# Tile 0 of a fused attention and feed-forward kernel split into 6 and 10 slices instead of 8 and 8

## The chip, the cores and the metric

The kernel runs on one core of a Trainium2 chip. The metric is the device time of one execution in microseconds (us). A core has a matrix engine (TensorE, PE in the profile, with its weight loads as PEld), a vector engine (VectorE, DVE), an engine for activation functions and copies (ScalarE, ACT), a general engine (GpSimd, POOL) and a queue that issues all transfers here (SyncE, SP). Each works through its own instructions in order and waits on semaphores for the others. PE writes into eight PSUM banks.

## The reference, cut to what matters

```python
# attention: 8 batches, 8 heads, 576 positions, 64 wide, float32
scores = q @ k.transpose / sqrt(64)
scores = where(mask, scores, -1e9)     # heads 0-3: the last 32 keys; heads 4-7: every 4th of the last 128
attn = exp(scores - max); attn = attn / (sum + 1e-9)
x = (attn @ v)                          # laid out as (4608 tokens, 512)
# feed-forward, w_in (512, 2048) and w_out (2048, 512) in float64
h = x @ w_in
g = max(h, 0) + alpha * min(h, 0)
out = g @ w_out                         # float32
```

Products run at float32 accuracy on PE by splitting each operand into a high and a low part: three passes (high by high, high by low, low by high) in place of one. The float64 weights are turned into such pairs of float32 on the core.

## The kernel before, in words

**Tiles, slices, pairs, chunks.** The 4608 tokens are nine tiles of 512. The 2048 hidden features are 16 slices of 128. For tile t and slice f, `ffn_h` (12 matmuls, L340) makes h, an activation makes g, and `ffn_y` (12 matmuls, L387) adds g times a slice of w_out into four PSUM banks `y`, one for each block of 128 outputs. Attention goes by pairs of heads: four pairs a batch, `pairs[0]` to `pairs[31]`. A pair's steps are `scores` (72 small matmuls, L185), `maxima` (DVE, L193 and L196), `exponentials` (ACT, nine, L203), `divisions` and `turns` (DVE, L210 to L218), `values` (76 small matmuls, L231), then `highs` (ACT) and `lows` (DVE), which put x in its tile as high and low part. Batches are 576 tokens, so that tile 0 needs the four pairs of batch 0, and tile 1 those of batches 0 and 1. A chunk is one slice of w_in or w_out, 512 KB as float64: `load_weight` on SP's queue, `magnitude` on ACT (L307), four `words` on DVE (L313 to L319), `high` on ACT (L325) and `low` on DVE (L328). There are 32, in the order of the list `wq`; `load` and `conversion` take the next of it.

**Stages.** Each engine's order is that in which the code below emits. (1) L784 to L853: the first loads, the four pairs of batch 0 (loop over `s`), with one chunk converted a round, and the start of tile 0. (2) The loop over `n` up to `CUT`, 8: tile 0's slices 0 to 7, with the four pairs of batch 1 and pairs of chunks; a pair's scores and maxima stand in one slice and its division in the next, so that a pair takes two slices. Seventeen chunks are through when it ends. The half sums of tile 0 go to memory (`part`). (3) The loop from `CUT` to `NS` (48): tile 1's 16 slices, with one chunk each, then tile 0's slices 8 to 15, then tile 2 in two halves. Slice n emits h of the slice after it and y of the slice before it. From slice 20 on every second slice scores a pair of batch 2 and later; from slice 24 (`SECOND`) the weights are saved to memory (`save`), and POOL adds up parts of them (`combine`, L431 and L434) in the space of tile 1's x, at its first call from slice 25, once tile 1's last h has read that space. At slice 32 tile 0's second half ends: the four partial sums are loaded, added on DVE (L395) and written out. (4) `paired_stage`: tiles 3 to 8 by twos, from about 370 us on.

**Activation.** `ffn_relu` (ACT, two operations, L348 and L349) and `ffn_sum` (DVE, L354) up to tile 1's end; after that `ffn_parts` (two DVE operations, L361 and L362). `ffn_high` and `ffn_low` split g.

**Shared space.** Scores, values and h take the four PSUM banks `a0` to `a3` in turn, so that a bank is free again when what it held four banks ago has been read. `y` takes the other four. Staged chunks and g share five buffers by turns (`gbuf`); chunks 4 to 15 are staged where the weights of slices 8 and 9 will lie, and the pairs of batches 0 and 1 lie where those of slices 10 to 15 will. Activations, magnitudes and outputs share five buffers with the tag `m`.

Of the kernel before, what the change touches and what calls it, by code (L numbers as in the profile page):

```python
# [37 lines left out]
CUT = 8  # L38
# [12 lines left out]
def tile_window_attention_prelu_ffn(  # L51
# [49 lines left out]
    SPANS = ((0, CUT), (CUT, CUT + 2), (CUT + 2, NF))  # L101
# [177 lines left out]
    def load_weight(which, f):  # L279
        i = order[which, f]  # L280
        if NC <= i < 2 * CUT:
            st = spare_st[i % 4]
        else:
            st = gbuf([P, DM, 2], U32, f"ws{which}_{f}")
# [7 lines left out]
    class Conversion:  # L292
# [7 lines left out]
        def magnitude(self):  # L300
            i = self.index
            if NC <= i < 2 * CUT and i % 2 == 0:
                self.a = spare_a[i // 2 % 2]
            else:
                self.a = ffp.tile([P, DM], U32, tag="m", name=f"wa{self.id}", bufs=5)

            nc.scalar.activation(out=self.a.bitcast(F32), in_=self.st[:, :, 1].bitcast(F32), func=AF.Abs)  # L307
# [66 lines left out]
    def ffn_y(t, f):  # L374
        first = (t, f) in ((0, 0), (0, CUT), (1, 0), (2, CUT))
# [4 lines left out]
        last = cut or (t, f) in ((0, NF - 1), (1, NF - 1), (2, CUT - 1))  # L380
# [10 lines left out]
        if not last:  # L391
            return
        for c in range(NC):
            if rest:
                nc.vector.tensor_tensor(out=o[c], in0=ys[t][c], in1=o[c], op=ALU.add)  # L395
            elif c % 2:
                nc.vector.tensor_copy(out=o[c], in_=ys[t][c])
            else:
                nc.scalar.copy(out=o[c], in_=ys[t][c])  # L399
            nc.sync.dma_start(  # L400
                out=part[c] if cut else outT[c * P:(c + 1) * P, t * TT:(t + 1) * TT], in_=o[c])
# [393 lines left out]
    pairs[3].load_v()  # L795
    pairs[0].scores()
    pairs[1].scores()
    for s in range(NC):
# [3 lines left out]
        if s == 0:  # L802
# [6 lines left out]
            for op in w.words():  # L809
                op()  # L810
        else:
# [20 lines left out]
    v.maxima(w.words())  # L832
    now = [conversion(), conversion()]
    words = [op for ops in zip(*(w.words() for w in now)) for op in ops]
    for op in words[:4]:
        op()
# [5 lines left out]
    for op in words[4:]:  # L842
        op()
    w.high()
    w.low()
# [11 lines left out]
    score_at = {2 * i + 1: pairs[NC + 1 + i] for i in range(NC - 1)}  # L857
    turn_at = {2 * i: pairs[NC + i] for i in range(NC)}
    value_at = {2 * i + 1: pairs[NC + i] for i in range(NC)}
    for p in range(2 * NC, AHEAD):  # L860
        n = EARLY + 2 * (p - 2 * NC)
        score_at[n] = pairs[p]
        turn_at[n + 2] = pairs[p]
        value_at[n + 3 if p == 2 * NC else n + 2] = pairs[p]
    divide_at = {n + 1: u for n, u in score_at.items()}

    for n in range(CUT):


        scored, valued, turned = score_at.get(n), value_at.get(n), turn_at.get(n)  # L870
        words = [op for ops in zip(*(w.words() for w in now)) for op in ops]
# [4 lines left out]
        if n + 1 == CUT:  # L876
            ffn_y(*slices[n - 1])
        if n == 0:
            for f in range(2):
                ffn_sum(*slices[f])  # L880
        elif turned:
            ffn_sum(*slices[n])
        ffn_high(*slices[n])
        if turned:
            turned.divisions()
            turned.turns()
        for w in late:
            w.low()
        if scored:
            scored.maxima([lambda: ffn_low(*slices[n])] + words)  # L890
            ffn_h(*slices[n + 1])
            scored.exponentials(0, 4)
            valued.highs()
            scored.exponentials(4)
            valued.lows()
        else:
            if valued:
                valued.highs()
                valued.lows()
            if n:  # L900
                ffn_h(*slices[n + 1])
            ffn_low(*slices[n])
            for op in words[:4]:
                op()
        following = None
        if turned:
            following = [conversion() for _ in range((2, 2, 2, 1, 0, 0, 1, 1)[n])]
            if n:

                ffn_relu(*slices[n + 1])  # L910
                ffn_sum(*slices[n + 1])
            for op in words[4:]:
                op()
        elif not scored:
            for op in words[4:]:
                op()
        late = now
        for _ in range((2, 2, 1, 0, 0, 1, 1, 1)[n]):
# [154 lines left out]
```

## Time and profile before

| what | us |
|---|---|
| median of 3 runs (901.9 to 904.94) | 902.15 |
| the profiled execution, its own time | 903.91 |
| its span | 901.0 |
| busy in the span: PE / DVE / ACT / POOL | 855.4 / 561.2 / 395.6 / 48.1 |
| mean clock granted to PE | 0.981 |

In the lists of the profile a row of a timeline gives the start in us from the span's beginning, the length, the engine, the line in the kernel, the operation with what it writes and reads, and in brackets the idle time ahead of it with what ended it. Neighbouring instructions are merged (x12), and lengths of merged rows overlap the next by the pipeline's depth; differences of starts are the better prices. A row of busy times gives a stretch, then its length and the busy time of each engine, then the granted clock (1.00 is full speed), the share of transfers and GB/s.

### The profile page before, as it was taken

What the parts mean: (1) busy time and instruction counts of PE and PEld (TensorE: products, weight loads), DVE (VectorE), ACT (ScalarE), POOL (GpSimd) and SP (SyncE); (2) the same over time, 40 slices, a digit from 0 to 9 for tenths busy, and PEclk for the clock granted to TensorE, in tenths of its full rate; (3) what the DMA queues carried; (4) which work ended last, traced back from release to release, by engine and by line L of the source; (5) the groups of instructions that cost most, each with busy time, mean ns of one, the idle gap of its engine ahead of it and who ended that gap; (6) DMA issues with size and microseconds to landing.
All of it is one profiled execution on the core that took longest, in us unless ns stands there. A gap on an engine that the chain in (4) does not pass through costs nothing.

```text
span 901.0 us, 19714 instructions
## 1 busy us (share of the span) xinstructions
PE 855.4 (95%) x8048; PEld 706.7 (78%) x8048; DVE 561.2 (62%) x962; ACT 395.6 (44%) x1122; POOL 48.1 (5%) x52
## 2 busy tenths in 40 slices
PE   4659999989998999999999999999999999999998
PEld 4547788868887878888888888888788888888886
DVE  5999688786666767676436666664357527404731
ACT  4666555534434354464335642563356216303610
POOL 0000000030222432000000000000000000000000
PEclk9769999998999999999999999999999999999999
DMA  9632253214798976475557565665466467435641
GB/s 331 217 130 79 70 172 102 95 54 155 225 305 255 305 230 191 165 201 151 165 167 194 173 199 159 203 176 142 115 179 173 140 175 193 135 94 166 185 129 47
DMA packets 101305, 151.82 MB, mean 168 GB/s; under 512 B 8416, under 2 KB 47328, under 8 KB 101216
## 3 DMA queue, kind: packets, MB, share of 16 engines
q1 hardware_dynamic: 101216, 150.58, 55.5%
q8 instruction: 63, 1.03, 0.5%
q14 instruction: 26, 0.21, 0.1%
HBM read 116.99 MB, written 33.55 MB: 167 GB/s over the span
## 4 chain that ended last, share of the span: by engine, by line
PE 87%; DVE 7%; ACT 2%; issue 1%; DMA 1%; SPq 1%; DVEq 0%; ACTq 0%
PE y L670 29%; PE pA L532 15%; PE h L340 13%; PE y L387 12%; PE pC L532 7%; PE o L231 4%; PE pB L532 4%; PE s L185 3%; DVE w_dt.float32r L328 1%; ACT w_dt.float L203 1%; DMA mask_sb<-masks 1%; DVE pt L218 1%; DVE wa L317 1%; DVE g L372 1%; DMA ob<-part 1%
## 5 line engine op out<-in xcount | busy, mean ns | idle before, releaser
L340 PE MATMUL h<-x,w_dt.float32r 128*128 128x512 f32 x576 | 146.5, 405 | 10.4 <-DVE w_dt.float L193 6.2
L387 PE MATMUL y<-g,w_dt.float32r 128*128 128x512 f32 x576 | 140.7, 394 | 0.0
L340 PEld LDWEIGHTS h<-x,w_dt.float32r 128*128 128x128 f32 x576 | 110.9, 195 | 35.1 <-DVE w_dt.float L193 6.5
L387 PEld LDWEIGHTS y<-g,w_dt.float32r 128*128 128x128 f32 x576 | 109.2, 190 | 23.5 <-ACT ob L399 0.4
L670 PE MATMUL y<-gp,ring_w 128*128 128x512 f32 x480 | 112.3, 391 | 0.0
L670 PEld LDWEIGHTS y<-gp,ring_w 128*128 128x128 f32 x480 | 89.8, 188 | 18.8
L670 PE MATMUL y<-gp,ring_xA 128*128 128x512 f32 x444 | 103.8, 391 | 0.0
L670 PEld LDWEIGHTS y<-gp,ring_xA 128*128 128x128 f32 x444 | 83.1, 188 | 17.5
L203 ACT ACTIVATE pr<-pr,nm 128x64 f32<-128x64 f32 x216 | 72.2, 336 | 47.7 <-DVE nm L196 47.7
L574 ACT COPY stage<-pA 128x512 f32<-128x512 f32 x72 | 42.3, 588 | 105.2 <-PE pA L532 105.2
L600 DVE TENSOR_TENSOR gp<-n,gp 128x512 fp32r<-128x512 f32 x96 | 63.2, 684 | 0.0
L592 DVE SCALAR_TENSOR_TENSOR n<-n,bal,stage 128x512 f32<-128x512 f32 x72 | 54.0, 749 | 13.9 <-ACT n L588 13.1
L367 ACT CAST g<-m 128x512 fp32r<-128x512 f32 x48 | 29.8, 621 | 68.7 <-DVE m L362 61.0
L532 PE MATMUL pA<-parts_w,ring_w 128*128 128x512 f32 x234 | 57.7, 390 | 0.8 <-ACT raw_xA L267 0.8
L596 ACT CAST gp<-n 128x512 fp32r<-128x512 f32 x96 | 56.6, 615 | 1.9 <-DVE n L592 1.9
L532 PE MATMUL pA<-parts_w,ring_xA 128*128 128x512 f32 x228 | 56.2, 390 | 0.5 <-ACT raw_xB L267 0.5
L670 PE MATMUL y<-gp,ring_g 128*128 128x512 f32 x228 | 54.5, 392 | 0.0
L693 DVE TENSOR_TENSOR ob<-y,py 128x512 f32<-128x512 f32 x24 | 16.4, 691 | 57.8 <-PE y L670 57.8
L532 PEld LDWEIGHTS pA<-parts_w,ring_w 128*128 128x128 f32 x234 | 43.9, 188 | 9.9 <-ACT raw_xA L267 0.9
L588 ACT ACTIVATE n<-stage 128x512 f32<-128x512 f32 x72 | 45.6, 634 | 12.5 <-DVE stage L581 12.0
L532 PEld LDWEIGHTS pA<-parts_w,ring_xA 128*128 128x128 f32 x228 | 42.7, 188 | 9.4 <-ACT raw_xB L267 0.6
L670 PEld LDWEIGHTS y<-gp,ring_g 128*128 128x128 f32 x228 | 42.5, 188 | 9.1
(97 smaller groups left out, 1148.8 us busy)
## 6 DMA issues: line engine op xcount, KB each, us to landing
ring_w<-wS SPq DMA_DIRECT2D x68, 256.0 KB, 2.9
ring_xA<-wS SPq DMA_DIRECT2D x67, 256.0 KB, 2.9
ring_w<-wO SPq DMA_DIRECT2D x40, 256.0 KB, 2.8
ring_xA<-wO SPq DMA_DIRECT2D x37, 256.0 KB, 2.8
out<-ob SPq DMA_DIRECT2D x36, 256.0 KB, 3.0
ring_g<-wS SPq DMA_DIRECT2D x33, 256.0 KB, 2.9
wO<-w_dt.float32r SPq DMA_DIRECT2D x32, 256.0 KB, 4.7
wS<-wc SPq DMA_DIRECT2D x16, 512.0 KB, 3.4
```

The source lines that it names most:

```text
L203: nc.scalar.activation(out=self.pr[:, r, :], in_=self.pr[:, r, :], func=AF.Exp, bias=self.nm[:, r:r + 1], scale=1.0, accum_out=self.sm[:, ...
L231: nc.tensor.matmul(self.po[u][e * D:(e + 1) * D, a:z, :], lhsT=self.v[rows, i, :], rhs=self.pt[rows, a * BK + (BQ if i else 0):z * BK - (B ...
L340: nc.tensor.matmul(ms[t, f], lhsT=weight(0, a, f)[:, c * P:(c + 1) * P], rhs=half(t, c)[:, e, :], start=(c == 0 and n == 0), stop=(c == NC ...
L367: nc.scalar.copy(out=g[:, 0, :], in_=ms[t, f])
L387: nc.tensor.matmul(ys[t][c], lhsT=weight(1, a, f)[:, c * P:(c + 1) * P], rhs=g[:, e, :], start=(first and n == 0), stop=(last and n == 2),)
L532: nc.tensor.matmul(to, lhsT=w[:, (2 * a + c) * P:(2 * a + c + 1) * P], rhs=part_of(name, e)[:, c * TT:(c + 1) * TT], start=start and c == ...
L574: nc.scalar.copy(out=self.s(n), in_=self.A)
L588: nc.scalar.activation(out=self.m[n], in_=self.at(n), func=AF.Relu, scale=-1.0)
L592: nc.vector.scalar_tensor_tensor(out=self.m[n], in0=self.m[n], scalar=bal[:, f:f + 1], in1=self.at(n), op0=ALU.mult, op1=ALU.add)
L596: nc.scalar.copy(out=self.g(n)[:, 0], in_=self.m[n])
L600: nc.vector.tensor_tensor(out=g[:, 1], in0=self.m.pop(n), in1=g[:, 0].bitcast(F32), op=ALU.subtract)
L670: nc.tensor.matmul(ys2[tt], lhsT=w[:, k * P:(k + 1) * P], rhs=g[:, e], start=j == 0 and n == 0, stop=j == GF - 1 and n == 2)
```

## The change

`CUT` becomes 6, and `HALF` = 8 takes its place wherever 8 stood for the storage of the weights, for tile 2's halves, for the saves and POOL's sums (`SCRATCH`), and for the first load of batch 2. So slices 0 to 5 are tile 0's first part, 6 to 21 tile 1, 22 to 31 tile 0's other ten; from slice 24 the slice numbers of saves, sums and pairs are those of before.

- The first chunk is loaded right behind the first pair's q and k and converted ahead of the first maxima; the masks come in two transfers, the second ahead of pair 3.
- The loop over tile 0's first slices is written anew: slice n scores pair 5 + n, takes its maxima, exponentials, division and turn, and slice n + 1 has its values. Chunks are taken by the list `taken`, one or two a slice; `ahead` loads what the next slice will convert. Before tile 1, 13 chunks' words are through; the 19 others fall in slices 6 to 19.
- The copies or additions at the end of a part of a tile are kept as `end` in the list `ended` and emitted behind the maxima and the first five exponentials of the slice's pair.

The diff; lines that are only "..." stand for what is left out, most of the old loop's body among it:

```diff
-CUT = 8
+HALF = 8
+CUT = 6
...
-        if NC <= i < 2 * CUT:
+        if NC <= i < 2 * HALF:
...
-            if NC <= i < 2 * CUT and i % 2 == 0:
+            if NC <= i < 2 * HALF and i % 2 == 0:
...
-        first = (t, f) in ((0, 0), (0, CUT), (1, 0), (2, CUT))
+        first = (t, f) in ((0, 0), (0, CUT), (1, 0), (2, HALF))
...
         cut, rest = (t, f) == (0, CUT - 1), t == 0 and f == NF - 1
-        last = cut or (t, f) in ((0, NF - 1), (1, NF - 1), (2, CUT - 1))
+        last = cut or (t, f) in ((0, NF - 1), (1, NF - 1), (2, HALF - 1))
...
-        if not last:
-            return
-        for c in range(NC):
-            if rest:
-                nc.vector.tensor_tensor(out=o[c], in0=ys[t][c], in1=o[c], op=ALU.add)
-            elif c % 2:
-                nc.vector.tensor_copy(out=o[c], in_=ys[t][c])
-            else:
-                nc.scalar.copy(out=o[c], in_=ys[t][c])
-            nc.sync.dma_start(
-                out=part[c] if cut else outT[c * P:(c + 1) * P, t * TT:(t + 1) * TT], in_=o[c])
+
+        def end():
+            for c in range(NC):
+                if rest:
+                    nc.vector.tensor_tensor(out=o[c], in0=ys[t][c], in1=o[c], op=ALU.add)
+                elif c % 2:
+                    nc.vector.tensor_copy(out=o[c], in_=ys[t][c])
+                else:
+                    nc.scalar.copy(out=o[c], in_=ys[t][c])
+                nc.sync.dma_start(
+                    out=part[c] if cut else outT[c * P:(c + 1) * P, t * TT:(t + 1) * TT], in_=o[c])
+
+        if last:
+            ended.append(end)
+
+    ended = []
...
-    slices += [(2, f) for f in range(CUT, NF)] + [(2, f) for f in range(CUT)]
+    slices += [(2, f) for f in range(HALF, NF)] + [(2, f) for f in range(HALF)]
     NS = len(slices)
     SECOND = CUT + NF
+    SCRATCH = HALF + NF
...
-    wq = [(0, 0), (0, 1), (0, 2), (1, 0)]
-    for f in range(1, CUT):
-        wq += [(0, f + 2), (1, f)] if f + 2 < CUT else [(1, f)]
-    wq.append((0, CUT))
-    for f in range(CUT, NF):
+    wq = [(0, 0), (0, 1), (1, 0)]
+    for f in range(1, NF):
         wq += [(0, f + 1), (1, f)] if f + 1 < NF else [(1, f)]
...
+    def masks_of(kind):
+        nc.sync.dma_start(out=mask_sb[:, kind:kind + HB], in_=masks[:, kind:kind + HB])
+
     pairs[0].load_qk()
-    nc.sync.dma_start(out=mask_sb, in_=masks)
     load()
+    masks_of(PLAIN)
     nc.sync.dma_start(out=al, in_=alpha)
     pairs[1].load_qk()
+    load()
     pairs[0].load_v()
-    for i in (2, 3):
-        pairs[i].load_qk()
-        load()
-        pairs[i - 1].load_v()
+    pairs[2].load_qk()
     load()
+    pairs[1].load_v()
+    masks_of(DILATED)
+    pairs[3].load_qk()
+    load()
+    pairs[2].load_v()
     pairs[3].load_v()
     pairs[0].scores()
     pairs[1].scores()
+    before = conversion()
+    for op in before.words():
+        op()
+    before.high()
...
             for op in w.words():
                 op()
+            before.low()
...
-    v.maxima(w.words())
...
+    v.maxima()
     u.highs()
     v.exponentials(0, 4)
     u.lows()
     for f in range(2):
         ffn_h(0, f, NC - 1, NC)
-    for op in words[4:]:
+    for op in w.words():
         op()
-    w.high()
-    w.low()
     ffn_relu(0, 0)
     v.exponentials(4)
     ffn_relu(0, 1)
-    for _ in range(3):
-        load()
-    late, now = now, [conversion(), conversion()]
-    for w in late:
-        w.high()
-
-
-
...
+    w.high()
+    load()
+    late, now = [w], [conversion()]
+
+    taken = [1, 2, 1, 1, 1, 2] + [1, 1, 2, 1, 1, 1, 2, 1, 1, 2, 1, 2, 1]
+
+    def ahead():
+        while taken and len(convs) - taken[0] < len(loads):
+            load()
 
...
     for n in range(CUT):
...
+        scored = pairs[NC + 1 + n] if n + 1 < NC else None
+        valued = pairs[NC + n] if n < NC else None
+        if n == 0:
+            for f in range(2):
+                ffn_sum(*slices[f])
+            valued.divisions()
+            valued.turns()
+        elif n > 1:
+            ffn_sum(*slices[n])
         if scored:
             scored.scores()
         if valued:
             valued.values()
...
+        if n:
+            ffn_h(*slices[n + 1])
         ffn_high(*slices[n])
...
+        if scored:
+            scored.maxima()
+            scored.exponentials(0, 5)
+        ffn_low(*slices[n])
+        if valued:
+            valued.highs()
+        if scored:
+            scored.exponentials(5)
+        if n:
+            ffn_relu(*slices[n + 1])
+        for w in now:
+            for op in w.words():
+                op()
+        if valued:
+            valued.lows()
         for w in late:
             w.low()
         if scored:
-            scored.maxima([lambda: ffn_low(*slices[n])] + words)
...
+            scored.divisions()
+            scored.turns()
+        for w in now:
             w.high()
...
+        late, now = now, [conversion() for _ in range(taken.pop(0))]
+        ahead()
+        if n:
             ffn_y(*slices[n - 1])
...
-        n = SECOND + 1 + 2 * k + (2 if k > 1 else 0)
+        n = SCRATCH + 1 + 2 * k + (2 if k > 1 else 0)
...
-        whole = n + 1 == SECOND + CUT
+        whole = n + 1 == 2 * NF
...
-            for w in now:
-                load()
             if n + 1 <= SECOND - 2:
                 ffn_relu(*slices[n + 1])
-            late, now = now, [conversion()] if convs else []
+            late, now = now, [conversion() for _ in range(taken.pop(0) if taken else 0)]
+            ahead()
             for w in late:
                 w.high()
...
         if scored:
             scored.maxima()
             scored.exponentials(0, 5)
+        while ended:
+            ended.pop()()
         if valued and valued is not pairs[2 * NC]:
...
-                due = n == CUT + 3, n == CUT + 3
+                due = n == HALF + 3, n == HALF + 3
...
-        if SECOND <= n < SECOND + NF:
-            save(n - SECOND)
+        if SCRATCH <= n < SCRATCH + NF:
+            save(n - SCRATCH)
         if n in combine_at:
-            combine(combine_at[n], "xB1" if n < SECOND + 5 else "xA1")
+            combine(combine_at[n], "xB1" if n < SCRATCH + 5 else "xA1")
...
     ffn_y(*slices[-1])
+    ended.pop()()
```

More of the change, by code (lines that the diff above doesn't have):

```diff
@@ L97, in gbuf @@
         return ffp.tile(shape, dtype, tag=f"g{i}", name=name, bufs=1)
-    SPANS = ((0, CUT), (CUT, CUT + 2), (CUT + 2, NF))
+    SPANS = ((0, HALF), (HALF, HALF + 2), (HALF + 2, NF))
     places = {}
@@ L831, in tile_window_attention_prelu_ffn @@
     ffn_h(0, 1, 0, NC - 1)
-    v.maxima(w.words())
[L833 to L836, printed above, removed]
+    v.maxima()
     u.highs()
@@ L848, in tile_window_attention_prelu_ffn @@
     ffn_relu(0, 1)
-    for _ in range(3):
-        load()
-    late, now = now, [conversion(), conversion()]
-    for w in late:
-        w.high()
[L857 to L865, printed above, removed]
-    for n in range(CUT):
-        scored, valued, turned = score_at.get(n), value_at.get(n), turn_at.get(n)
-        words = [op for ops in zip(*(w.words() for w in now)) for op in ops]
+    w.high()
[5 more added lines that the diff above has]
+            load()
+    for n in range(CUT):
+        scored = pairs[NC + 1 + n] if n + 1 < NC else None
[7 more added lines that the diff above has]
+            ffn_sum(*slices[n])
         if scored:
@@ L875, in tile_window_attention_prelu_ffn @@
             valued.values()
[L876 to L882, printed above, removed]
-        ffn_high(*slices[n])
-        if turned:
-            turned.divisions()
-            turned.turns()
+        if n:
+            ffn_h(*slices[n + 1])
+        ffn_high(*slices[n])
+        if scored:
[13 more added lines that the diff above has]
+            valued.lows()
         for w in late:
@@ L889, in tile_window_attention_prelu_ffn @@
         if scored:
-            scored.maxima([lambda: ffn_low(*slices[n])] + words)
[L891 to L918, printed above, removed]
-            load()
-        if not turned and n < CUT - 1:
-            ffn_relu(*slices[n + 1])
-        for w in late:
+            scored.divisions()
+            scored.turns()
+        for w in now:
             w.high()
-        now = following if turned else [conversion() for _ in range((2, 2, 2, 1, 0, 0, 1, 1)[n])]
-        if 0 < n < CUT - 1:
+        late, now = now, [conversion() for _ in range(taken.pop(0))]
+        ahead()
+        if n:
             ffn_y(*slices[n - 1])
-    ffn_relu(*slices[CUT])
+    score_at, value_at = {}, {}
+    for p in range(2 * NC, AHEAD):
+        n = EARLY + 2 * (p - 2 * NC)
+        score_at[n] = pairs[p]
+        value_at[n + 3 if p == 2 * NC else n + 2] = pairs[p]
+    divide_at = {n + 1: u for n, u in score_at.items()}
     split_at, combine_at = {}, {}
     for k in range(NFP):
-        n = SECOND + 1 + 2 * k + (2 if k > 1 else 0)
+        n = SCRATCH + 1 + 2 * k + (2 if k > 1 else 0)
         combine_at[n] = (k + NFP // 2) % NFP
@@ L954, in tile_window_attention_prelu_ffn @@
                 op()
-            for w in now:
-                load()
             if n + 1 <= SECOND - 2:
                 ffn_relu(*slices[n + 1])
-            late, now = now, [conversion()] if convs else []
+            late, now = now, [conversion() for _ in range(taken.pop(0) if taken else 0)]
+            ahead()
             for w in late:
```

## The prediction

> **What bounds the kernel now.** I read the page first, then busy times by stage, then the timelines of the stages in which TensorE (PE) is not full.
>
> ```profile
> PE 855.4 (95%) x8048; PEld 706.7 (78%) x8048; DVE 561.2 (62%) x962; ACT 395.6 (44%) x1122; POOL 48.1 (5%) x52
> ```
>
> The next rows are the busy-time view; after the stretch come its length and the busy us of PE, PEld, DVE, ACT and POOL, then the granted clock.
>
> ```profile
> 0.00:92.40 92.40, 60.08 (x1229) 50.25 (x1229) 79.74 (x171) 55.32 (x197) 0.20 (x4) 0.87 0.56 190
> 92.40:197.90 105.50, 105.50 (x666) 86.21 (x664) 79.34 (x139) 54.61 (x128) 6.49 (x6) 1.00 0.31 99
> ...
> 370.00:901.00 531.00, 526.00 (x3952) 434.61 (x3950) 280.69 (x442) 214.72 (x533) 0.00 (x0) 1.00 0.56 160
> ```
>
> PE idles 901.0 - 855.4 = 45.6 us. Of that 32.3 lie before 92.4, where VectorE (DVE) is busy for 79.7 us and PE waits for it; 4.2 lie at the end of tile 1 and 2.6 where tile 0's second part ends (rows 202.10 and 273.87 below). From 370 on nothing is touched. The matmuls are the same before and after, so the change can only move idle time and half-clock time in these three places.
>
> **The head, to the point where PE stays full.** The next rows are DVE's timeline: start, us, operation, idle before.
>
> ```profile
> 8.28 0.49 DVE L193 SCALAR_TENSOR_TENSOR w_dt.float<-s,mask_sb 128x320 f32<-128x320 f32 x1 [8.28 <-DMA mask_sb<-masks]
> ...
> 9.99 0.17 DVE L807 TENSOR_SCALAR nal<-al 128x16 f32<-128x16 f32 x1
> ...
> 11.01 0.43 DVE L313 TENSOR_SCALAR wa<-wa 128x512 f32<-128x512 f32 x1 [0.78 <-ACT wa L307]
> ...
> 13.27 0.16 DVE L210 TENSOR_SCALAR rs<-sums 128x9 f32<-128x9 f32 x1
> ...
> 15.21 0.65 DVE L328 TENSOR_TENSOR w_dt.float32r<-wa,w_dt.float32r 128x512 fp32r<-128x512 f32 x1
> 15.78 0.48 DVE L193 SCALAR_TENSOR_TENSOR w_dt.float<-s,mask_sb 128x320 f32<-128x320 f32 x1
> ...
> 39.02 0.48 DVE L193 SCALAR_TENSOR_TENSOR w_dt.float<-s,mask_sb 128x320 f32<-128x320 f32 x1
> ...
> 48.59 0.74 DVE L354 SCALAR_TENSOR_TENSOR m<-m,nal,h 128x512 f32<-128x512 f32 x1
> 50.13 0.75 DVE L354 SCALAR_TENSOR_TENSOR m<-m,nal,h 128x512 f32<-128x512 f32 x1 [0.80 <-ACT h L349]
> ...
> 53.91 0.69 DVE L372 TENSOR_TENSOR g<-m,g 128x512 fp32r<-128x512 f32 x1
> ...
> 65.69 0.89 DVE L272 TENSOR_TENSOR x<-o,x 128x288 fp32r<-128x288 f32 x3
> ...
> 94.72 1.36 DVE L272 TENSOR_TENSOR x<-o,x 128x224 fp32r<-128x224 f32 x4 [0.67 <-ACT x L267]
> ```
>
> Start to start these are DVE's prices: a pair's maxima 9.99 - 8.28 = 1.7; a chunk's four words 13.27 - 11.01 = 2.27; division and turn 15.21 - 13.27 = 2.0; a chunk's low half 0.57; a slice's sum and its low half some 0.65 each without their overlap; a pair's low halves 0.8 or 1.3.
>
> First term: the first chunk now stands ahead of the masks in SP's queue and ahead of the first maxima on DVE. Before, the masks, third in that queue, landed at 8.2. I estimate that the chunk, nearly as large and in the same place, lands then too; with ACT's magnitude (some 0.7) its words run from 8.9 to 11.2, and the maxima start at 11.2 instead of 8.28. A second chunk's words follow as before, and the first chunk's low half (0.57) is added. The second pair starts at 15.78 + 2.95 + 0.57, 3.5 later, less what the shorter mask transfer gives back: I take 3.3. The rounds after it have the same instructions, so that pair 4's maxima start at 42.3 instead of 39.02. The second half of the masks, a transfer of its own on SP, is wanted only from pair 2 on. What keeps its slice number (saves, POOL's sums, batch 2's loads, all still counted from 8) keeps its place in SP's and POOL's queues.
>
> Second term: the way into tile 0. PE and ACT there:
>
> ```profile
> 37.99 2.42 PE L231 MATMUL o<-pt,w_dt.float 32*64 32x32 f32 x76 [5.33 <-issue]
> 40.34 6.70 PE L340 MATMUL h<-x,w_dt.float32r 128*128 128x512 f32 x18
> 49.39 1.21 PE L185 MATMUL s<-w_dt.float 64*32 64x64 f32 x72 [2.34 <-DVE m L354]
> 52.87 2.34 PE L231 MATMUL o<-pt,w_dt.float 32*64 32x32 f32 x76 [2.28 <-DVE pt L218]
> 60.18 5.29 PE L340 MATMUL h<-x,w_dt.float32r 128*128 128x512 f32 x12 [4.97 <-DVE w_dt.float L193]
> 65.31 2.90 PE L387 MATMUL y<-g,w_dt.float32r 128*128 128x512 f32 x12
> 68.05 2.88 PE L340 MATMUL h<-x,w_dt.float32r 128*128 128x512 f32 x12
> ...
> 91.08 1.35 PE L231 MATMUL o<-pt,w_dt.float 32*64 32x32 f32 x76 [1.39 <-DVE m L354]
> ```
> ```profile
> 46.38 0.60 ACT L348 ACTIVATE m<-h 128x512 f32<-128x512 f32 x1 [2.67 <-PE h L340]
> ```
>
> Pair 3's values start 3.3 later (41.3), and PE needs the same 46.38 - 37.99 = 8.4 us at half clock up to the first relu: 49.7. DVE before filled this stretch with the words of three chunks; now only one chunk's words stand there, end at 47.7, and DVE waits for the relu. The sums run at 50.8 and 53.4 (before 48.59 and 50.13) and end at 54.1: some 4.8 us of DVE idle time that was not there.
>
> Third term: the slices. Slice 0 on DVE: divide and turn 2.0, maxima 1.7, low 0.6, one chunk 2.27, low halves 0.8 and 0.6, divide and turn 2.0: it ends at 64.1. Slice 1 has the same without the first 2.0: 72.1. Slice 2 has sum 0.7, maxima 1.7, low 0.6, two chunks 4.5, low halves 1.3 and 0.6, divide and turn 2.0, and a wait: its scores stand on PE behind slice 1's values, h and y. PE idles 3.5 us before those values (64.1), so they run at half clock as in the rows 52.87 and 60.18. It lasts 5.1 us from 60.18 to 65.31 and some 6 after 202.10 (below: 2.35 and 4.91 hold 3.0 us too much); I take 5.4. Values 2.4, h 4.2, y 2.72 (65.31 to 68.05), scores 1.2: at 74.65. Maxima that could have begun at 72.8 begin then, 1.85 later. The last pair's turn ends at 85.4.
>
> Fourth term: from 85.4 PE has all it needs (the weights' low halves are at least 1.5 us ahead, ACT has room). It has then done 4 h, 2 y and 7 values; before, at 91.08 where its last gap of the head ends, 6 h, 4 y and 6 values. So it has 4 x 2.72 - 1.35 = 9.5 us more ahead of it: 94.9 against 91.1, 3.8 later. It idles 4.05 us before this point, which gives half clock again (values 2.4 for 1.35, 3 us of h at half speed: 2.6 lost): **6.4 us later**.
>
> ```profile
> 274.00:276.00 2.00, 2.00 (x5) 0.50 1.01 292
> ```
>
> How long a gap brings half clock: in the trace 2.58 us did (this row follows the gap at 271.3), 1.39 did not (row 91.08); a gap of 4.05 lies well past it. [...]
>
> Bounds of the head: if neither gap brings half clock, 1.85 and 2.6 fall away, and 1.9 is left. If the first chunk lands 2 us later than the masks did and both recoveries take the 6 us of row 202.10, it is 9. I take 5.6, a little under the sum, since the gaps were found by adding up and any reserve in the queues shortens them.
>
> **Tile 1.** Nineteen chunks in 14 slices where before it was one in each:
>
> ```profile
> 150.00:178.69 28.69, 28.69 (x129) 23.75 (x127) 21.95 (x39) 13.47 (x25) 0.00 (x0) 1.00 0.32 108
> ...
> 174.63 0.75 DVE L354 SCALAR_TENSOR_TENSOR m<-m,nal,h 128x512 f32<-128x512 f32 x1 [0.94 <-ACT h L349]
> ```
>
> DVE is busy 21.95 / 28.69 x 5.44 = 4.16 us a slice, 1.3 of it for the slice itself; with 19/14 chunks it is 1.3 + 1.36 x 2.87 = 5.2 against 5.44 of PE. A slice with two chunks takes 7.0 and falls back 1.6 us; y stands four PE groups (10.9 us) behind its h and wants some 3 of them, so this is hidden. Loads are made for the next slice's conversions; each has a slice of 5.44 to land. Cost 0, bounds 0 and 3 (DVE stops some 3 us for the buffers of the partial sums at the end of part one, as before).
>
> **End of tile 1.** Timelines of DVE, POOL and PE:
>
> ```profile
> 191.63 1.46 DVE L328 TENSOR_TENSOR w_dt.float32r<-wa,w_dt.float32r 128x512 fp32r<-128x512 f32 x1
> 193.02 1.50 DVE L313 TENSOR_SCALAR wa<-wa 128x512 f32<-128x512 f32 x1
> ...
> 201.56 0.48 DVE L193 SCALAR_TENSOR_TENSOR pr<-s,mask_sb 128x320 f32<-128x320 f32 x1
> ```
> ```profile
> 191.25 2.98 POOL L431 TENSOR_TENSOR wsum_xB<-w_dt.float32r 128x512 f32<-128x512 f32 x2 [190.81 <-PE h L340]
> 194.31 3.96 POOL L434 TENSOR_TENSOR wsum_xB<-wsum_xB 128x256 f32<-128x256 f32 x4
> ```
> ```profile
> 202.10 2.35 PE L231 MATMUL o<-pt,v 32*64 32x32 f32 x76 [4.17 <-DVE pr L193]
> 204.37 4.91 PE L387 MATMUL y<-g,w_dt.float32r 128*128 128x512 f32 x12
> ```
>
> POOL's sums start when tile 1's last h is done. While they run DVE's words take 1.50 instead of 0.43, DVE falls behind, and pair 9's maxima free the PSUM bank for pair 8's values only at 202. Now tile 1's last h is at slice 20, the last words are at 19, and pair 9's maxima stay at 22: while POOL runs DVE has one sum, one low half and pair 8's maxima, some 4 us even stretched by half. Gain: the gap 4.17, values 2.35 - 1.35, y 4.91 - 2.9: **7.2 us**. Bounds 3 (half the lag stays) and 7.2. The copies of tile 1's results now stand behind pair 9's maxima and five exponentials; scores, h and values on PE (5.3 us) hide them.
>
> **End of tile 0.** The chain of waits, DVE and PE:
>
> ```profile
> 265.94 4.73 DMA ob<-part
> ```
> ```profile
> 270.76 2.66 DVE L395 TENSOR_TENSOR ob<-y,ob 128x512 f32<-128x512 f32 x4 [0.46 <-DMA ob<-part]
> 273.33 0.48 DVE L193 SCALAR_TENSOR_TENSOR pr<-s,mask_sb 128x320 f32<-128x320 f32 x1
> ```
> ```profile
> 273.87 4.33 PE L340 MATMUL h<-x,w_dt.float32r 128*128 128x512 f32 x12 [2.58 <-DVE pr L193]
> ```
>
> The four additions wait for the partial sums to land and hold up pair 14's maxima, whose bank the next h wants. The change puts the additions behind the maxima: these start at 270.2, and h follows the values at 271.3. Additions from 272.0 free one bank each 0.65 us, the next y starts at 274.0 and takes 0.68 a bank. Gain 2.58 + 4.33 - 2.9 = **4.0**; bounds 2.6 and 4.0.
>
> **Sum.** 5.6 - 7.2 - 4.0 = -5.6. The profiled execution took 903.91 around its span of 901.0, the runs' median is 902.15, their lowest 901.9; from the median: 896.5.
>
> **Rivals.** A, *the head costs little* (half clock stays away, the first chunk lands early): 1 - 11.2 is 10 us off, 892. For it: the gaps of 3.5 and 4.05 hang on sums of small terms. Against: the gaps of 2.58, 4.17, 4.97 and 5.33 us in the rows above are all followed by matmuls at half clock.
> B, *a stall comes back elsewhere*: the deferred copies or additions hold y's banks, or POOL still hits DVE; one of the two gains is lost: 5.6 - 4 to 7.2 is between +1.6 and -1.6, so 902. Against: 5.3 us of cover at both places.
> C, *slower: VectorE becomes the bound of tile 1*. Had DVE in each slice the wait of 0.94 that row 174.63 shows, and a like one of 0.3 ahead of the low half, it would need 6.45 us a slice; 14 x (6.45 - 5.44) = 14.1, less some 5 of slack, is +9: 902.15 - 5.6 + 9 = 905.6; with the head at its upper bound 909. It decides from 6.2 us a slice on. Against: DVE waits there because it is early, and loses these waits as soon as it is late.
>
> **How the numbers follow.** The forecast has 0.55, A 0.20, B 0.16, C 0.09. About 0.5% (4.5 us) is what a measurement of this kernel can tell from no change. The forecast's own range, 891 to 901, lies for two thirds below 897.6: 0.37 faster and 0.18 within. A is faster. B gives 0.12 within and 0.04 faster. C gives 0.08 slower and 0.01 within. Faster 0.61, same 0.31, slower 0.08. Low end 889: the head at its bound of 1.9 and both gains whole give 892.9, and the 3.3 of the start would vanish as well if the first chunk landed well ahead of the masks' 8.2. High end 903: B and the mild side of C.
>
> **What would show it.** DVE's second round starts near 19 instead of 15.78; the two sums of tile 0's first slices near 51 and 53.5 with idle time before them; PE gaps of 3 to 5 us near 61 and 81 with a clock of 0.5 after them; PE full from some 85 on; no gap before pair 8's values and none behind the partial sums' landing. It is wrong if tile 1 shows PE idle, if DVE has no idle time near 48, or if gaps remain at the ends of tile 1 and tile 0.

## The result, and the profile after

| kernel | median, us | lowest to highest | runs |
|---|---|---|---|
| before | 902.02 | 901.56 to 904.94 | 4 |
| changed | 895.25 | 893.61 to 895.52 | 4 |

The ratio is 0.9925, with a 95% interval of 0.9902 to 0.9949. The forecast was 896.5. The profiled execution of the changed kernel took 895.02 around a span of 892.9, which is 8.1 less than the span of before. One execution each of two kernels below took 1231.62 and 2984.44 us, and their medians and ratios leave these out.

The busy-time view of the changed kernel, in the columns explained with the profile of before. Most of its lines in kernel.py are one higher than before (h is L341, y L388, scores L186, values L232).

```profile
0.00:92.40 92.40, 61.11 (x1292) 52.19 (x1293) 74.43 (x161) 53.50 (x211) 0.20 (x4) 0.82 0.51 173
92.40:190.00 97.60, 97.60 (x498) 80.69 (x497) 85.62 (x151) 55.87 (x111) 5.75 (x6) 1.00 0.37 119
```

PE is full from 92.4 to 190 though VectorE's share there has risen to 85.62 / 97.60 = 88%. The head up to 92.4 has nearly the PE time of before (61.11 against 60.08).

**The head.** VectorE's timeline of the changed kernel: the first chunk's words, the second pair's maxima, the first two sums of tile 0 and the maxima of its slice 2.

```profile
6.80 0.43 DVE L314 TENSOR_SCALAR wa<-wa 128x512 f32<-128x512 f32 x1 [6.80 <-ACT wa L308]
...
17.15 0.48 DVE L194 SCALAR_TENSOR_TENSOR w_dt.float<-s,mask_sb 128x320 f32<-128x320 f32 x1
...
47.84 0.75 DVE L355 SCALAR_TENSOR_TENSOR m<-m,nal,h 128x512 f32<-128x512 f32 x1 [1.91 <-ACT h L350]
...
50.47 0.75 DVE L355 SCALAR_TENSOR_TENSOR m<-m,nal,h 128x512 f32<-128x512 f32 x1 [1.89 <-ACT h L350]
...
70.67 0.49 DVE L194 SCALAR_TENSOR_TENSOR w_dt.float<-s,mask_sb 128x320 f32<-128x320 f32 x1 [1.15 <-PE s L186]
```

PE in the same stretch, and the h that follows the y of tile 1's first slice:

```profile
61.12 2.34 PE L232 MATMUL o<-pt,w_dt.float 32*64 32x32 f32 x76 [3.49 <-issue]
63.40 3.79 PE L341 MATMUL h<-x,w_dt.float32r 128*128 128x512 f32 x12
...
81.47 1.82 PE L232 MATMUL o<-pt,w_dt.float 32*64 32x32 f32 x76 [3.47 <-issue]
83.22 4.10 PE L341 MATMUL h<-x,w_dt.float32r 128*128 128x512 f32 x12
87.16 2.88 PE L388 MATMUL y<-g,w_dt.float32r 128*128 128x512 f32 x12
...
111.64 2.65 PE L341 MATMUL h<-x,w_dt.float32r 128*128 128x512 f32 x11
```

The same h in the kernel before:

```profile
121.54 2.69 PE L340 MATMUL h<-x,w_dt.float32r 128*128 128x512 f32 x11
```

Tile 1 now starts two slices earlier, and two slices are 2 x 5.44 = 10.88 us of PE. With equal work done, 111.64 stands against 121.54 - 10.88 = 110.66: the head costs **1.0** in this pair of profiles, where 5.6 was forecast. That is the low end of what this head costs: in six profiles, this one and those of five of the kernels below, that share its first transfers, the words begin between 6.80 and 8.61, and 6.80 is the earliest. In the kernel with the end emitted at once, whose head is the same, they begin at 7.55, and the y that stands at 87.16 here starts at 88.39.

**End of tile 1.** PE and POOL of the changed kernel, and two VectorE instructions that run beside POOL's:

```profile
198.81 1.35 PE L232 MATMUL o<-pt,v 32*64 32x32 f32 x76
```
```profile
179.89 2.55 POOL L437 TENSOR_TENSOR wsum_xB<-w_dt.float32r 128x512 f32<-128x512 f32 x2 [179.45 <-PE h L341]
182.52 3.27 POOL L440 TENSOR_TENSOR wsum_xB<-wsum_xB 128x256 f32<-128x256 f32 x4
```
```profile
180.63 0.69 DVE L363 SCALAR_TENSOR_TENSOR m<-h,m 128x512 f32<-128x512 f32 x1
182.01 0.98 DVE L373 TENSOR_TENSOR g<-m,g 128x512 fp32r<-128x512 f32 x1 [0.69 <-ACT g L368]
```

No gap ahead of pair 8's values, and they take 1.35 and not 2.35, so no half clock either: **-7.2**. Of VectorE's work only L373 is stretched (0.98 for 0.65 to 0.69), and POOL's own sums are shorter too, 2.55 and 3.27 where they were 2.98 and 3.96.

**End of tile 0.**

```profile
263.75 1.35 PE L232 MATMUL o<-pt,v 32*64 32x32 f32 x76
265.04 3.02 PE L341 MATMUL h<-x,w_dt.float32r 128*128 128x512 f32 x12
```

Values and the next h follow each other; the gap of 2.58 and the half clock are gone: **-4.0**.

**After that.** A place in the paired stage that both kernels reach with the same work, and a gap behind it, first in the changed kernel, then the same place before:

```profile
458.96 1.65 PE L538 MATMUL pA<-parts_w,ring_xA 128*128 128x512 f32 x6 [0.50 <-ACT raw_xB L268]
...
526.38 0.86 PE L186 MATMUL s<-k,q 64*32 64x64 f32 x45 [1.30 <-issue]
```
```profile
468.95 1.66 PE L532 MATMUL pA<-parts_w,ring_xA 128*128 128x512 f32 x6 [0.50 <-ACT raw_xB L267]
```

At this place the changed kernel is 468.95 - 458.96 = 10.0 ahead, and 1.0 - 7.2 - 4.0 = -10.2. From here to the end it loses 1.9 again, 1.30 of it in the gap at 526, for which the trace shows no wait. So -8.1 in this pair of executions is +1.0 - 7.2 - 4.0 and some 2 us at places that the change doesn't touch.

### The profile page after: what moved, and what is told of

Read it like the earlier page. It is cut to its first block, busy times and chain, and to the rows that moved or that the text cites. A ratio compares the mean times of both kernels' runs of the same rounds, so it can differ in the third digit from the quotient of the medians.

```text
span 892.9 us, 19710 instructions
## 1 busy us (share of the span) xinstructions
PE 853.4 (96%) x8048; PEld 706.5 (79%) x8048; DVE 561.3 (63%) x964; ACT 394.3 (44%) x1118; POOL 46.9 (5%) x52
## 4 chain that ended last, share of the span: by engine, by line
PE 94%; DVE 2%; issue 2%; ACT 1%; DMA 0%; SPq 0%; DVEq 0%; ACTq 0%
PE y L676 30%; PE h L341 15%; PE pA L538 15%; PE y L388 15%; PE pC L538 7%; PE o L232 5%; PE pB L538 4%; PE s L186 3%; ACT w_dt.float L204 1%; DMA ws<-w_in 0%; DVE pt L219 0%; DVE w_dt.float L213 0%; DVE w_dt.float32r L329 0%; DVE nm L197 0%; DVE wa L318 0%
## 5 line engine op out<-in xcount | busy, mean ns | idle before, releaser
L341 PE MATMUL h<-x,w_dt.float32r 128*128 128x512 f32 x576 | 144.4, 400 | 1.6 <-issue 1.6
L388 PE MATMUL y<-g,w_dt.float32r 128*128 128x512 f32 x576 | 138.4, 389 | 0.0
L341 PEld LDWEIGHTS h<-x,w_dt.float32r 128*128 128x128 f32 x576 | 109.6, 193 | 25.2 <-issue 1.8
L388 PEld LDWEIGHTS y<-g,w_dt.float32r 128*128 128x128 f32 x576 | 108.0, 188 | 22.5
```

The costliest lines, as they stand in the source:

```text
L341: nc.tensor.matmul(ms[t, f], lhsT=weight(0, a, f)[:, c * P:(c + 1) * P], rhs=half(t, c)[:, e, :], start=(c == 0 and n == 0), stop=(c == NC ...
L388: nc.tensor.matmul(ys[t][c], lhsT=weight(1, a, f)[:, c * P:(c + 1) * P], rhs=g[:, e, :], start=(first and n == 0), stop=(last and n == 2),)
```

## The experiments

The theory after the result: the whole gain is two stalls, POOL's sums beside VectorE's conversions at the end of tile 1 and the additions ahead of pair 14's maxima at the end of tile 0; the new head and the spread chunks bring nothing by themselves, and the head's price hangs on when the first chunk lands. Rivals: the spread chunks gain of themselves; only one of the two stalls counts; the late 2 us belong to the change. Three groups of kernels ran, each on its own chip beside the kernel before, whose medians there were 902.26, 901.86 and 903.06. Times are compared by ratio to it.

### The changed kernel with the end of a tile emitted at once

```diff
         if last:
-            ended.append(end)
+            end()
...
-        while ended:
-            ended.pop()()
...
-    ended.pop()()
```

> The changed kernel, but copies and additions at a part's end stand right behind y again, ahead of the pair's maxima. Theory (each of three places is worth what its own rows say: head +1 us, end of tile 1 -7.2, end of tile 0 -4.0): the gap ahead of h of slice (2,10) comes back with half clock after it, +4.0 us: 899.3; nothing else changes. Rival (the partial sums land early enough now that the order on VectorE no longer matters): 895.3. Second rival (the order also mattered at the end of tile 1): 902 or more.

Measured: 897.78, ratio 0.9960 (0.9941 to 0.9979), where the changed kernel has 0.9925: by the ratios the deferral is worth 3.2 us, where 4.0 was expected. PE at the end of tile 0, and the busy-time view of that h:

```profile
268.68 3.02 PE L341 MATMUL h<-x,w_dt.float32r 128*128 128x512 f32 x12 [2.34 <-DVE pr L194]
```
```profile
268.68:271.70 3.02, 3.02 (x13) 2.52 (x14) 1.65 (x5) 2.46 (x14) 0.00 (x0) 1.00 1.00 322
```

The gap is back in its old place. But the clock stays at 1.00 behind it, while before it fell to 0.50 after 2.58: of the 4.0, the gap is there each time (2.34 here, 2.58 before, 1.86 with POOL kept back), and the half clock's 1.4 in one execution and not in another.

### The kernel before with only the end of a tile deferred

```diff
-        if not last:
-            return
-        for c in range(NC):
+        def end():
+            for c in range(NC):
...
+        if last:
+            ended.append(end)
...
+        while ended:
+            ended.pop()()
...
+    ended.pop()()
```

> The kernel before, with only the deferral of copies and additions behind the pair's maxima and five exponentials. Theory: only the gap at 271 goes, 2.6 us and 1.4 us of half clock: 902.0 - 4.0 = 898.0; the 4.2 us gap at 198 stays. Rival (the deferral is what cured the end of tile 1 as well): 891.

Measured: 899.16, ratio 0.9980 (0.9960 to 1.0000): some 1.8 us by the ratio, at most 3.6, and 3.1 by the medians, where 4.0 was expected. The gap of tile 0 is gone, the other stands where it was:

```profile
201.03 2.35 PE L231 MATMUL o<-pt,v 32*64 32x32 f32 x76 [4.16 <-DVE pr L193]
...
269.40 3.02 PE L340 MATMUL h<-x,w_dt.float32r 128*128 128x512 f32 x12
```

The place is right and the two stalls are separate. The price of 4.0 stands in the pair of profiles and lies above this interval.

### The kernel before with POOL kept back

An addition on POOL of 0.32 us that reads pair 10's divided scores stands ahead of the first weight sum, so that the sums can't start when tile 1's last h is done, but only some 25 us later (at 216.40, before at 191.25). It adds work and changes no result.

```diff
         t = sums_at[tag]
+        if not gated:
+            gated.append(1)
+            nc.gpsimd.tensor_tensor(out=idle, in0=pr0[:, 0, :], in1=pr0[:, 1, :], op=ALU.add)
```

> The kernel before, with one small addition (128x64, result unused) ahead of GpSimd's first weight sum, which reads pair 10's probabilities and so keeps GpSimd's first sums back until some 222 us; VectorE's instructions are those of before. Theory (GpSimd's sums slow VectorE's words down and make pair 9's maxima late): words stay at 0.42 and 0.69 us, the gap ahead of pair 8's values shrinks from 4.2 to under 1 us, the clock stays full: 902.0 - 7.2 = 895, at least -4. Rival (VectorE has too much of its own to do there: a chunk, the last activation, a pair): the gap stays at over 3 us, 902.

Measured: 897.3, ratio 0.9939 (0.9917 to 0.9961), 5.5 us. PE, then VectorE in the stretch in which POOL used to run:

```profile
198.23 1.35 PE L231 MATMUL o<-pt,v 32*64 32x32 f32 x76 [0.40 <-DVE pr L193]
...
266.38 4.59 PE L340 MATMUL h<-x,w_dt.float32r 128*128 128x512 f32 x12 [1.86 <-DVE pr L193]
```
```profile
192.15 0.42 DVE L313 TENSOR_SCALAR wa<-wa 128x512 f32<-128x512 f32 x1
```

The same chunk is converted at the same place; its first word takes 0.42 where the prediction's row has 1.50, and of the gap of 4.17 0.40 is left. So it was POOL, and not how many chunks stood there. In this profile the place itself gives 4.17 - 0.40 for the gap, 1.0 for the values and 1.9 for y, together 6.7; elsewhere half clock takes some of it back (the h at 310.60 takes 4.25, the same h before 2.68, both shown at the end). At tile 0's end 1.86 us of idleness were enough for half clock (h 4.59).

Not every VectorE instruction beside POOL is stretched: of the two rows of the changed kernel shown above, L363, with one input in a PSUM bank (h), takes its usual 0.69, and L373, whose two inputs (m and g) lie in none, takes 0.98 instead of 0.65 to 0.69. By what means POOL stretches the one and not the other, no run here shows.

### The changed kernel with parts of 8 and 8

`CUT` alone goes back, and `taken` with it so that tile 1 has a chunk a slice; the new order of the head and the deferral stay.

```diff
-CUT = 6
+CUT = 8
...
-    taken = [1, 2, 1, 1, 1, 2] + [1, 1, 2, 1, 1, 1, 2, 1, 1, 2, 1, 2, 1]
+    taken = [2, 2, 2, 1, 1, 1, 1, 1] + [1] * 14
```

> The changed kernel with tile 0 in parts of 8 and 8 again (the other edits kept; 17 chunks converted ahead of tile 1, one a slice after). Theory (tile 1's last h, and with it GpSimd's first sums, must come after the last words): they meet again at slice 22, the gap ahead of pair 8's values is back at some 4 us: 895.3 + 7.2 = 902.5, the head the same within 2 us. Rival (the new loop itself or the deferral cured it): 895 to 897.

Measured: 903.1, ratio 1.0009 (0.9993 to 1.0025). PE and VectorE at the end of tile 1:

```profile
205.92 2.35 PE L232 MATMUL o<-pt,v 32*64 32x32 f32 x76 [4.16 <-DVE pr L194]
```
```profile
196.84 1.50 DVE L314 TENSOR_SCALAR wa<-wa 128x512 f32<-128x512 f32 x1
```

The gap (4.17 before) and the stretched word (1.50) are back. Without the split the other parts gain nothing in sum. The difference to the changed kernel is 0.0084 x 902 = 7.6, against 7.2 forecast, but it is no clean price of this stall: the values behind the gap stand at 205.92 where before has 202.10, so that this kernel's head costs 3.8 and not within 2 of the changed kernel's 1.0, and the gap of 1.56 that before has at 317.84 is only 0.35 here.

### The changed kernel with the whole masks ahead of the first chunk

```diff
     pairs[0].load_qk()
+    nc.sync.dma_start(out=mask_sb, in_=masks)
     load()
-    masks_of(PLAIN)
...
-    masks_of(DILATED)
```

> The changed kernel with the order of transfers of before at the start: the whole masks ahead of the first chunk. VectorE's order stays that of the change. Theory (the head up to the last pair is a chain on VectorE, and a later first chunk delays all of it): the chunk lands some 2 us later than in the changed kernel, its words start near 8.9 instead of 6.8, the last pair's values near 83.5 instead of 81.5: +2.0, 897.3. Rival (VectorE's idle times near 47 and 49 take it up, since PE sets the way into tile 0): under +0.7, at most 896.

Measured: 898.24, ratio 0.9962 (0.9944 to 0.9981), by the ratios 3.3 above the changed kernel where 2.0 was expected. VectorE's first word, the second round, and PE's last gap of the head:

```profile
9.30 0.43 DVE L314 TENSOR_SCALAR wa<-wa 128x512 f32<-128x512 f32 x1 [9.30 <-ACT wa L308]
...
19.66 0.48 DVE L194 SCALAR_TENSOR_TENSOR w_dt.float<-s,mask_sb 128x320 f32<-128x320 f32 x1
```
```profile
84.84 1.50 PE L232 MATMUL o<-pt,w_dt.float 32*64 32x32 f32 x76 [3.47 <-issue]
```

The words start 2.5 later than in the changed kernel, the second round 2.5 and the last values 3.4 later. Nothing on the way takes up a late start. This is close to the head that was forecast: words from 8.9, a second round at 19.1, the last turn at 85.4. In the execution of the kernel with the end emitted at once, whose head is the changed kernel's own, the words begin at 7.55 and the last values stand at 82.72: the chunk's landing differs from one execution to the next.

### The changed kernel with one h computed twice

h of slice 3 is computed a second time over the first, with the same result: 12 matmuls, some 2.7 us, put where PE has 3.5 us of idleness.

```diff
-    def ffn_h(t, f, first=0, end=NC):
-        if first == 0:
+    def ffn_h(t, f, first=0, end=NC, again=False):
+        if first == 0 and not again:
...
         if n:
             ffn_h(*slices[n + 1])
+        if n == 2:
+            ffn_h(*slices[n + 1], again=True)
```

> The changed kernel with h of tile 0's slice 3 computed twice (12 more matmuls, the second 12 start the sum anew, so the result is the same), which fills most of the 3.5 us in which PE waits for the last pair's turn. Theory (that gap costs half clock afterwards): the gap falls to 0.8 us, values take 1.35 instead of 1.8 and the next h 2.9 instead of 4.1: -1.6, 893.7. Rival (the clock falls anyway or had not cost anything): 895.3; if the doubled h delays y and with it the pair, up to 896.5.

Measured: 897.02, ratio 0.9945 (0.9923 to 0.9967), not better than the changed kernel, and 3.3 above the 893.7 that was expected. PE in the head, and its two gaps of over 1 us behind it:

```profile
81.84 1.35 PE L232 MATMUL o<-pt,w_dt.float 32*64 32x32 f32 x76 [0.73 <-issue]
...
280.34 4.26 PE L341 MATMUL h<-x,w_dt.float32r 128*128 128x512 f32 x11 [2.42 <-issue]
...
518.05 4.43 PE L676 MATMUL y<-gp,ring_xA 128*128 128x512 f32 x12 [1.88 <-issue]
```

In the head it does what was expected: the gap is 0.73, the values take 1.35 and the h after them 3.06, so the clock stays up. But the gap that the other kernels have near 307 is now at 280 and longer, with half clock behind it, and there is one at 518. The gain in the head is offset there: with twelve more matmuls the gaps for which the trace shows no wait stand at other places (more on these at the end).

### The changed kernel with a seventh chunk's words early

The idle 1.91 and 1.89 of VectorE are filled with the words of the next chunk.

```diff
     for op in w.words():
         op()
+    more = conversion()
+    for op in more.words():
+        op()
     ffn_relu(0, 0)
     v.exponentials(4)
     ffn_relu(0, 1)
     w.high()
+    more.high()
     load()
-    late, now = [w], [conversion()]
+    late, now = [w, more], [conversion()]
...
-    taken = [1, 2, 1, 1, 1, 2] + [1, 1, 2, 1, 1, 1, 2, 1, 1, 2, 1, 2, 1]
+    taken = [1, 1, 1, 1, 1, 2] + [1, 1, 2, 1, 1, 1, 2, 1, 1, 2, 1, 2, 1]
```

> The changed kernel with the seventh chunk's words taken ahead of tile 0's first sum, where VectorE idles 1.9 us twice, so that slice 2 has one chunk's words in place of two. Theory (VectorE sets the last pair's turn; its idle times near 47 and 49 are wasted): the turn ends some 2 us earlier, the gap ahead of the last values falls to some 1.3 us and the clock stays full: -2 to -3.5, 892 to 893. Rival (PE's chain through slices 1 and 2 sets it: the pair's maxima waited 1.15 us for their scores): -0.5 or less, 895.

Measured: 892.67 (891.85 to 892.98), ratio 0.9891 (0.9864 to 0.9918). PE's last gap of the head:

```profile
82.70 1.35 PE L232 MATMUL o<-pt,w_dt.float 32*64 32x32 f32 x76 [1.22 <-issue]
83.98 3.02 PE L341 MATMUL h<-x,w_dt.float32r 128*128 128x512 f32 x12
86.84 2.88 PE L388 MATMUL y<-g,w_dt.float32r 128*128 128x512 f32 x12
```

The gap shrinks from 3.47 to 1.22 and the clock stays up, although the first chunk's words began at 8.61 in this execution and not at 6.80.

### The kernel before with both stalls removed

Deferral and POOL kept back together, in the kernel before: its old head, parts of 8 and 8, a chunk a slice. The edit is the two diffs above.

> The kernel before with the deferral and with GpSimd's first sums kept back, parts of 8 and 8 and the old head. Theory (the change's whole gain is these two gaps, and its head costs some 1 us): both gaps are gone, 902.3 - 3.1 - 5.5 = 893.7 by the two single runs, 891 by the rows; as fast as the changed kernel or a little faster. Rival (the gains overlap, or the gap only moves on): 897 to 899.

Measured: 892.77, ratio 0.9899 (0.9872 to 0.9925). PE at the two places:

```profile
198.50 1.35 PE L231 MATMUL o<-pt,v 32*64 32x32 f32 x76 [0.41 <-DVE pr L193]
...
264.74 3.02 PE L340 MATMUL h<-x,w_dt.float32r 128*128 128x512 f32 x12
```

Both gaps are gone. As fast as the changed kernel, with none of the new split: this carries the theory that the two stalls are the whole gain.

### The four closest on one chip

> The changed kernel as it is, beside the next three on one chip. My theory: its ratio to the kernel before stays within 0.990 to 0.995 (893 to 897.5 us), and which stretches have an instruction gap of 1.3 to 2.4 us past 268 us differs from the first profile of it; the gap before the last values of tile 0's part one stays near 3.5 us. Rival (the 2.05 us lost after 268 us belong to the change): the gap of 1.30 us before the scores at 526 us shows again, at the same place.

> The changed kernel with the seventh chunk's words ahead of tile 0's first sums, beside the changed kernel on the same chip. My theory: VectorE's idle time before the first two sums (1.91 and 1.89 us in the changed kernel) is what the head still loses, so this is 2 to 3 us faster than the changed kernel (the gap before the last values 1.2 us instead of 3.5, and h after it at 3.0 instead of 4.1). Rival (the first time of 892.67 was luck in the instruction gaps): the two agree within 1 us.

> The changed kernel with the seventh chunk's words early and h of slice 3 computed twice (the second time over the first, so the output is the same). The second h is 2.6 us of TensorE work. My theory: with the words early the gap that it would fill is only 1.2 us, so it costs more than it fills: 1 to 1.5 us slower than the kernel with the words early alone. Rival (keeping the clock up is worth more than the work): equal to it or faster.

> The kernel before with the end of a tile deferred and GpSimd's first sum kept back, with its old head and parts of 8 and 8, beside the changed kernel on the same chip. My theory: the two stalls are the whole gain and the changed kernel's head costs 1 us, so this is 0 to 2 us faster than the changed kernel and 0 to 2 us slower than the one with the words early. Rival (the 17 spread chunks or the new head bring a gain of their own): this is over 2 us slower than the changed kernel.

| kernel | median, us | ratio to before (95%) |
|---|---|---|
| changed | 894.36 | 0.9903 (0.9878 to 0.9928) |
| changed, seventh chunk's words early | 892.36 | 0.9885 (0.9860 to 0.9911) |
| that, with h of slice 3 twice as well | 896.86 | 0.9927 (0.9901 to 0.9954) |
| before, both stalls removed | 895.75 | 0.9920 (0.9897 to 0.9943) |

The words early are 2.0 us faster by the medians, the low end of what was expected, and 892.36 and 892.67 in the two groups are the lowest medians of all, if only just (892.77 for the kernel before with both stalls removed); four of the six runs of the second group lie below every run of the changed kernel, though the intervals of the ratios overlap. The second h costs 4.5, not 1 to 1.5. PE in that kernel:

```profile
282.19 3.77 PE L341 MATMUL h<-x,w_dt.float32r 128*128 128x512 f32 x10 [2.19 <-issue]
...
519.34 2.92 PE L676 MATMUL y<-gp,ring_xA 128*128 128x512 f32 x12 [1.60 <-issue]
```

The same two gaps as in the other kernel with 12 more matmuls: 2.7 us of work and a gap more account for most of the 4.5. The kernel before with both stalls removed was expected 0 to 2 faster than the changed one and is 1.4 slower, within what these runs can tell; the rival's bound (over 2 slower) isn't reached. PE there:

```profile
307.52 4.19 PE L340 MATMUL h<-x,w_dt.float32r 128*128 128x512 f32 x11 [1.82 <-issue]
...
527.47 0.87 PE L185 MATMUL s<-k,q 64*32 64x64 f32 x46 [1.05 <-issue]
```

The gap near 527 that cost the changed kernel 1.30 stands here too, without the new head or the new parts, and it isn't in the traces of the kernels with the words early. So the late loss comes neither from the new head nor from the new parts. Whether it comes with having both stalls gone stays open: no profile of a kernel that keeps a stall (before and the first four experiments) has a gap between 518 and 536, and five of the eight profiles without stalls have one. What was expected of the gaps in the repeat of the changed kernel stays untested.

## Why the prediction was right, point by point

**The time** came out 1.25 under the forecast, by two misses against each other, so that the closeness of the number is luck. In the pair of profiles the change is -8.1 where -5.6 was forecast: the head was 4.6 cheaper, and the late gaps took 1.9 back. By the medians it is -6.8, and -8.7 in the repeat.

**The first term, the start of the head**, was mis-sized. The estimate was that the first chunk lands when the masks did, at 8.2, with words from 8.9; in the profiled execution ACT had it at 6.10 and the words began at 6.80. From there on the working holds: second round forecast 19.1 - 8.9 = 10.2 behind the first word, measured 17.15 - 6.80 = 10.35. So the start cost 17.15 - 15.78 = 1.4, not 3.3. The kernel with the masks first, whose words began at 9.30, shows the forecast's size: its last values of the head stand at 84.84, 3.4 later than the changed kernel's. The landing itself is no fixed number: the words began at 6.80, 7.55, 7.61, 8.31, 8.53 and 8.61 in six executions of kernels whose first transfers are the same. All lie before the forecast's 8.9, so the term was too large; that the profiled execution has the earliest of them is luck.

**The second term** named the right wait, VectorE idle ahead of the first two sums, at 1.91 + 1.89 = 3.8 where 4.8 was forecast; the sums came at 47.84 and 50.47, 3 earlier than forecast, 2 of it from the start.

**The third and fourth terms** were right in mechanism: gaps of 3.49 and 3.47 before the values at 61.12 and 81.47 (forecast 3.5 and 4.05), half clock behind both, slice 2's maxima late by 1.15 (forecast 1.85). The half clock behind the last gap cost (83.22 - 81.47) + (87.16 - 83.22) = 5.69, against 4.14 in the kernel with the words early (82.70 to 86.84): 1.55, where 2.6 was put. The clock came back before h was through (0.69 granted over the values, 0.50 from 83.22 to 85.5, 0.99 from there to 87.16).

**Tile 1** at nothing was right: PE is full from 92.4 to 190 with VectorE at 88%. Rival C needed 6.2 us of VectorE a slice; 85.62 us over 97.6 / 5.44 = 17.9 slices is 4.8.

**The end of tile 1** was right in cause and price: -7.2 in the pair of profiles, about 7.6 by the kernel with parts of 8 and 8 (with 2.8 of a dearer head in it), 5.5 (3.5 to 7.5) by POOL alone kept back in the kernel before, where the place itself shows 6.7.

**The end of tile 0** was right in place; -4.0 stands in the pair of profiles, but the runs give 3.2 and 1.8 by their ratios, and behind the gap the half clock doesn't come each time. Rival B, a stall that comes back, is out: both gaps are gone, and each comes back when its own part of the change is undone. Rival A (892) had the size of the head's cost right, and of its two reasons the early chunk; the half clock did not stay away, as A had it, and the late gaps kept the time above 892.

**The late 1.9** stood nowhere in the forecast, which held that from 370 on nothing is touched. That is so for the work, not for the time: the gaps near 307 and 527 come and go or move by kernel and execution.

## What to carry to other kernels

A price of a stall is gap plus clock: where PE idles for some 2 us, count the gap in full and the half clock behind it as a chance (here the clock fell behind 2.58 and stayed at 1.00 behind 2.34), and keep both ends. When one engine's instructions grow to two or three times their length (here 0.69 to 1.46 and 0.42 to 1.50), look at what the neighbouring engine runs at that moment: here moving VectorE's conversions or POOL's sums out of each other's way was worth more than all the rest of the change. A first transfer's use began up to 1.8 us apart between executions here, and the chain of the head handed such a delay on in full (with the masks first, words 2.5 later and last values 3.4 later), so fill the stretch behind it with work that is wanted later (the seventh chunk's words) rather than with work that isn't (a second h).

## What the runs showed of the hardware that was not expected

**Half clock behind short gaps is not a matter of their length alone.** Behind gaps of 1.86 (before with POOL kept back, h 4.59), 1.82 (h 4.19 at 307.52) and 2.42 (h 4.26 at 280.34) h took 1.5 to 1.6 longer than the 3.02 at 268.68 (12 matmuls) and the 2.68 at 317.84 (11), both at a granted clock of 1.00. That is read here as half clock, since the h of 4.33 that follows the gap of 2.58 in the kernel before has 0.50 granted over 273.87 to 276.30. Behind 2.34 the clock did not fall, twice (h 3.02 at 268.68, and in the prediction's list the scores at 49.39, with a granted clock of 1.00). Two gaps of the same length at the same place of the work, first in the kernel before, then in the kernel before with POOL kept back:

```profile
317.84 2.68 PE L340 MATMUL h<-x,w_dt.float32r 128*128 128x512 f32 x11 [1.56 <-issue]
```
```profile
310.60 4.25 PE L340 MATMUL h<-x,w_dt.float32r 128*128 128x512 f32 x11 [1.56 <-issue]
```

The granted clock is 1.00 over the first of these h; the second takes 1.57 longer for the same 11 matmuls. What decides whether the clock falls behind such a gap, no run here shows.

**Gaps of PE for which the trace shows no wait.** Nearly every kernel has one of 1.3 to 1.9 us between 306 and 318, always behind the first or second matmul of an h; the kernel with parts of 8 and 8 has none there, and the kernels with 12 more matmuls have theirs at 280 to 282 and 518 to 519 instead. The transfers of the changed kernel ahead of the gap that ends at 307.83, by the transfer view of 304 to 306 us (queue, packets, MB, share of the 16 engines):

```profile
q1 hardware_dynamic: 905, 0.51, 88.7%
q8 instruction: 1, 0.02, 2.9%
```

A packet of instructions comes through right ahead of the gap, in a stretch in which the data queue takes 88.7% of the 16 engines. The page of the profile counts 63 such packets for the whole execution, before and after. Whether PE waits for such a packet there was not tried, and stays open. Other places in the changed kernel speak against a busy data queue beside the packet as the whole cause: such packets come between 292 and 294 us with the data queue at 84.7% and between 330 and 332 us with 99.3%, and PE's rows from 292.20 to 304.45 and from 329.31 to 342.85 follow each other without a gap; and ahead of the changed kernel's gap at 526 the packet comes between 523 and 525 us, where the data queue takes only 32.4%.
